# Attention by head pairs, with each pair's rows of the mode weights contracted beside the next pair's attention, and the mix packed by columns

## Chip, cores, metric

The kernel runs on one core of one Trainium2 chip. The metric is device time of one execution in microseconds (us), less is better. "Busy" times and waits come from one profiled execution each. A ratio is the mean time of one kernel's fast runs over the mean of the other's fast runs in the same rounds, so it is not quite the ratio of the medians that are quoted.

The engines are called as the profile calls them: PE (matmul), PEld (its weight load), DVE (vector), ACT (scalar, exponentials), POOL (GpSimd), SP (issues DMAs). "SPq" and "ACTq" are the instruction queues of SP and ACT that issue DMAs. SBUF is the on-chip memory that holds the tiles, PSUM the one that PE writes to here, in banks. The granted clock is the share of PE's full clock that the profile shows as granted in a stretch. The DMA share adds up the time of overlapping packets, so it can pass 1; it came to 1.24 where the weight stream ran steadily.

## The reference, cut to what matters

```python
# attention, 8 batches x 8 heads x 576 positions x 64, feature map of 2 x 128
def phi(x):
    proj = np.einsum('bhsd,df->bhsf', x, w_phi)
    proj = proj - np.max(np.abs(proj), axis=-1, keepdims=True)
    return np.concatenate([np.exp(proj), np.exp(-proj)], axis=-1)
kv  = np.einsum('bhsf,bhsd->bhfd', phi(k), v);  z = phi(k).sum(axis=2)
num = np.einsum('bhsf,bhfd->bhsd', phi(q), kv); den = phi(q) . z
x   = (num / den) as [batch, seq, head*64]          # D = 512

# spectral mix over x: 64 modes, one complex 512 x 512 matrix per mode
X = rfft(x, axis=1)[:, :64]
Y = X . (w_r + i w_i)            # per mode m: [8 batches, 512] x [512, 512]
u = x + irfft(Y);  out = u + relu(u @ w_ch)
```

The mode weights are 2 x 64 x 512 x 512 floats, 134 MB in fp32. Everything else that is read is about 29 MB.

## The kernel before

It has three stages. In the first, 32 units (one batch, two heads) go through attention; after a batch's last unit its Fourier transform is taken. Only when all heads of all batches are done can the mix of a mode start, since each mode needs all 512 rows of the spectrum. The mix loops over the modes, each with two weight transfers of 1 MB (read) and 16 matmuls with 8 stationary columns. The tail inverts the transform and multiplies by `w_ch`.

```python
units = [(b, g) for b in range(B_) for g in range(H_ // 2)]
for (ub, ug) in units:                     # skewed emission: front(n), back1(n-1), back2(n-2)
    f_q.append(frontA(ub, ug))
    if len(f_q) > 1: k_q.append(backA1(f_q.pop(0)))
    if len(k_q) > 1:
        st = k_q.pop(0); backA2(st)
        if st["h1"] == H_ - 1: rfftB1(st["b"])
...
for m in range(NMODES):
    wrr = pw.tile([128, 4, 512], BF16, tag="wrb")    # 6 buffers each
    wir = pw.tile([128, 4, 512], BF16, tag="wib")
    nc.gpsimd.dma_start(wrr, moe_w_r[m].rearrange("(dc p) e -> p dc e", p=128))
    nc.gpsimd.dma_start(wir, moe_w_i[m].rearrange("(dc p) e -> p dc e", p=128))
    ...                                              # 16 matmuls: [128 x 8].T @ [128 x 512]
    nc.scalar.copy(yst[:, 0, :], psYr); nc.vector.tensor_copy(yst[:, 1, :], psYi)
    nc.scalar.dma_start(yall[m:m + 1, :, :], yst[:, 0, :])
    nc.scalar.dma_start(yall[64 + m:65 + m, :, :], yst[:, 1, :])
```

The softmax here doesn't subtract the row's maximum and nothing guards it: scores larger than these inputs give would overflow.

## Time and profile before

Median 776.85 us (3 runs, 776.2 to 777.28).

| stage | us | what fills it |
|---|---|---|
| attention | 0 to about 390 | DVE 81%, ACT 76% busy (100 to 380 us); DMA share 0.33 |
| mix | 390 to 700 | weight stream at 207 GB/s; DVE 14%, ACT 12% |
| last rows of the mix | 700 to 703 | one transfer's landing |
| tail | 703 to 774 | PE 81%, DVE 78% |

The page of the kernel before: busy time of each engine; then the span in 40 slices, where a digit is the busy share in tenths (the rows of DVE and of the DMA), and GB/s moved; then the chain that ended last, by engine and by line.

```profile
PE 535.2 (69%) x3718; PEld 291.4 (38%) x3730; DVE 389.8 (50%) x896; ACT 322.3 (42%) x735; POOL 121.7 (16%) x173
...
DVE  5635889788878878787612111111111111116885
DMA  6899454544443421011089999999999999990445
GB/s 148 147 196 166 113 112 107 113 105 96 111 109 79 99 56 31 17 32 32 1 142 208 207 207 207 207 207 207 208 207 207 207 207 207 207 159 8 163 139 183
...
DMA 43%; issue 21%; PE 11%; DVE 10%; ACT 8%; SPq 5%; POOL 1%; DVEq 0%; POOLq 0%; ACTq 0%
DMA wrr<-in_moe_w_r_dram 36%; PE psf L421 3%; DMA qn<-in_q_dram 3%; DVE vaug L245 2%; DMA vn<-in_v_dram 2%; ACT AkBk L227 1%; ACT XT L322 1%; PE psN L208 1%; DVE ub L397 1%; ACT AkBk L222 1%; SPq L147 1%; DVE mk L214 1%; SPq L148 1%; PE psuT L407 1%; DMA out_dram<-of 1%
```

The two rows DVE and DMA are nearly complements: once DVE is at 7 to 8 tenths the DMA is at 5 tenths at most and falls to 0, and while the DMA is full DVE is at 1 or 2 tenths. The chain says the same: 36% of the span is waiting for weights.

The table of stages of the kernel before (start:end, length, then busy us and instruction count of PE, PEld, DVE, ACT, POOL, then granted PE clock, DMA share, GB/s):

```profile
core 0: us, PE busy (x) PEld busy (x) DVE busy (x) ACT busy (x) POOL busy (x), PEclk, DMA share, GB/s
100.00:380.00 280.00, 192.69 (x1922) 140.34 (x1925) 227.25 (x569) 212.11 (x517) 17.28 (x23) 0.77 0.33 75
400.00:680.00 280.00, 202.48 (x902) 74.10 (x899) 38.70 (x57) 32.55 (x57) 81.47 (x110) 1.00 1.24 207
703.00:774.00 71.00, 57.81 (x354) 29.35 (x360) 55.48 (x96) 13.95 (x24) 0.00 (x0) 0.96 0.38 134
```

In the middle row 280 us of the mix hold 38.7 us of DVE. GB/s counts what is written (bf16); twice that, 414 GB/s, is read.

### The profile page before, as it was taken

The page shows a single profiled execution, that of the slowest core. Times are in us where ns is not written, and L with a number is a line of the kernel's source. Part 1 is how long each engine was busy: PE and PEld are TensorE (multiplying, and loading weights), DVE is VectorE, ACT ScalarE, POOL GpSimd, SP SyncE. Part 2 cuts the span into 40 slices and gives each one's busy share as a digit, 9 for nine tenths or more (in the row PEclk, how much of TensorE's full clock was granted, in tenths as well). Part 3 has the DMA queues.
Part 4 walks back from the last instruction along what each step waited for, and adds up shares of the span by engine and source line. Part 5 has one row for each costly group of instructions (what it writes and reads, how often), then busy time and mean ns, then how long its engine had stood idle before and what let it go on. Part 6 is the DMA issues. An engine that isn't in the chain of part 4 may idle for free.

```text
span 774.3 us, 10671 instructions
## 1 busy us (share of the span) xinstructions
PE 535.2 (69%) x3718; PEld 291.4 (38%) x3730; DVE 389.8 (50%) x896; ACT 322.3 (42%) x735; POOL 121.7 (16%) x173
## 2 busy tenths in 40 slices
PE   1734776667667667776799776676677667667886
PEld 0422554545455444545533222222222222223443
DVE  5635889788878878787612111111111111116885
ACT  2844788877787877865411110110111011012220
POOL 1311010100100000000033323222232322200000
PEclk9855789887967887666599999999999999999999
DMA  6899454544443421011089999999999999990445
GB/s 148 147 196 166 113 112 107 113 105 96 111 109 79 99 56 31 17 32 32 1 142 208 207 207 207 207 207 207 208 207 207 207 207 207 207 159 8 163 139 183
DMA packets 192358, 107.74 MB, mean 139 GB/s; under 512 B 120496, under 2 KB 187184, under 8 KB 192304
## 3 DMA queue, kind: packets, MB, share of 16 engines
q0 software_dynamic: 67584, 67.12, 52.4%
q1 hardware_dynamic: 122672, 38.89, 20.9%
q10 hardware_dynamic: 2048, 1.05, 0.7%
q8 instruction: 29, 0.48, 0.2%
q14 instruction: 25, 0.20, 0.1%
HBM read 163.64 MB, written 9.44 MB: 224 GB/s over the span
## 4 chain that ended last, share of the span: by engine, by line
DMA 43%; issue 21%; PE 11%; DVE 10%; ACT 8%; SPq 5%; POOL 1%; DVEq 0%; POOLq 0%; ACTq 0%
DMA wrr<-in_moe_w_r_dram 36%; PE psf L421 3%; DMA qn<-in_q_dram 3%; DVE vaug L245 2%; DMA vn<-in_v_dram 2%; ACT AkBk L227 1%; ACT XT L322 1%; PE psN L208 1%; DVE ub L397 1%; ACT AkBk L222 1%; SPq L147 1%; DVE mk L214 1%; SPq L148 1%; PE psuT L407 1%; DMA out_dram<-of 1%
## 5 line engine op out<-in xcount | busy, mean ns | idle before, releaser
L384 DVE CAST yst<-psYi 8x512 bf16<-8x512 f32 x64 | 43.5, 679 | 272.7 <-PE psYi L378 272.7
L383 ACT CAST yst<-psYr 8x512 bf16<-8x512 f32 x64 | 36.8, 574 | 275.5 <-PE psYr L368 275.5
L363 PE MATMUL psYr<-wrr,XT 128*8 128x512 bf16 x256 | 66.5, 383 | 82.8 <-DMA wrr<-in_moe_w_r_dram 82.8
L257 PE MATMUL kvzT<-AkBk,vaug 128*65 128x128 bf16 x640 | 63.4, 257 | 22.1 <-DVE vaug L245 20.2
L359 POOL DMA_DIRECT2D wir<-in_moe_w_i_dram x64 | 47.5, 742 | 194.1 <-PE psYi L373 185.8
L368 PE MATMUL psYr<-wir,XT 128*8 128x512 bf16 x256 | 66.6, 383 | 0.0
L363 PEld LDWEIGHTS <-XT 128*8 128x8 bf16 x256 | 17.8, 86 | 129.2 <-DMA wrr<-in_moe_w_r_dram 109.5
L373 PE MATMUL psYi<-wir,XT 128*8 128x512 bf16 x256 | 65.9, 380 | 0.0
L378 PE MATMUL psYi<-wrr,XT 128*8 128x512 bf16 x256 | 65.7, 379 | 0.0
L257 PEld LDWEIGHTS <-vaug 128*65 128x65 bf16 x640 | 53.0, 137 | 29.1 <-DVE vaug L245 24.5
L173 PE MATMUL ptr<-ident_b,tb 128*128 128x128 bf16 x320 | 35.7, 255 | 40.6 <-POOL tb L168 26.1
L358 POOL DMA_DIRECT2D wrr<-in_moe_w_r_dram x64 | 47.6, 744 | 101.6 <-DMA wrr<-in_moe_w_r_dram 86.4
L168 POOL CAST tb<-qn 128x640 bf16<-128x640 f32 x32 | 24.5, 767 | 247.8 <-DMA qn<-in_q_dram 76.6
L214 DVE TENSOR_REDUCE mk<-psN 128x4 f32<-128x512 f32 (+1 forms) x96 | 52.3, 593 | 13.6 <-PE psN L208 13.5
L214 DVE TENSOR_REDUCE mq<-psN 128x4 f32<-128x512 f32 (+1 forms) x96 | 54.2, 581 | 8.3 <-PE psN L208 8.2
L222 ACT ACTIVATE AkBk<-psN 128x512 bf16<-128x512 f32 (+1 forms) x96 | 52.0, 541 | 5.2 <-DVE mk L214 5.2
L227 ACT ACTIVATE AkBk<-psN 128x512 bf16<-128x512 f32 (+1 forms) x96 | 53.0, 552 | 0.0
L173 PEld LDWEIGHTS <-tb 128*128 128x128 bf16 x320 | 27.3, 116 | 51.0 <-POOL tb L168 27.4
L296 DVE TENSOR_TENSOR tB<-psNB,e2mq 128x325 f32<-128x325 f32 x64 | 30.4, 493 | 20.9 <-PE psNB L291 19.6
L245 DVE TENSOR_TENSOR vaug<-vn,emm 128x650 bf16<-128x650 f32 x32 | 26.8, 838 | 24.6 <-ACT emm L239 24.3
L421 PE MATMUL psf<-wchb,uTb 128*128 128x512 bf16 x154 | 35.8, 379 | 0.6 <-DVE of L426 0.3
L368 PEld LDWEIGHTS <-XT 128*8 128x8 bf16 x256 | 22.4, 88 | 33.6 <-issue 1.2
(913 smaller groups left out, 971.7 us busy)
## 6 DMA issues: line engine op xcount, KB each, us to landing
wrr<-in_moe_w_r_dram POOLq DMA_DIRECT2D x64, 512.0 KB, 20.3
wir<-in_moe_w_i_dram POOLq DMA_DIRECT2D x64, 512.0 KB, 20.3
qn<-in_q_dram SPq DMA_DIRECT2D x64, 128.0 KB
kn<-in_k_dram SPq DMA_DIRECT2D x64, 128.0 KB
vn<-in_v_dram SPq DMA_DIRECT2D x64, 128.0 KB
out_dram<-of SPq DMA_DIRECT2D x32, 256.0 KB
yall<-yst ACTq DMA_DIRECT2D x128, 8.0 KB
wchf<-in_moe_w_ch_dram SPq DMA_DIRECT2D x1, 1024.0 KB
```

Of the source, the lines that this page charges most:

```text
L173: nc.tensor.transpose(ptr[:, c * 128:(c + 1) * 128], tb[:, c, :, :].rearrange("p h d -> p (h d)"), ident_b,)
L214: nc.vector.tensor_reduce(out=mm[:, :, 2 * cc:2 * cc + ncc].rearrange("p h c -> p c h"), in_=psN[:, 0:ncc, :].rearrange("p c (h f) -> p c ...
L222: nc.scalar.activation(AkBk[:, 2 * cc:2 * cc + ncc, :, 0, :], psN[:, 0:ncc, :].rearrange("p c (h f) -> p c h f", h=2), ACT.Exp, scale=1.0,)
L227: nc.scalar.activation(AkBk[:, 2 * cc:2 * cc + ncc, :, 1, :], psN[:, 0:ncc, :].rearrange("p c (h f) -> p c h f", h=2), ACT.Exp, scale=-1.0,)
L257: nc.tensor.matmul(kvzT[:, ab * 128:(ab + 1) * 128], lhsT=vaug[:, ab, c, hh, :], rhs=AkBk[:, c, hh, ab, :], start=(c == 0), stop=(c == NCH ...
L358: nc.gpsimd.dma_start(wrr, moe_w_r[m].rearrange("(dc p) e -> p dc e", p=128))
L359: nc.gpsimd.dma_start(wir, moe_w_i[m].rearrange("(dc p) e -> p dc e", p=128))
L363: nc.tensor.matmul(psYr, lhsT=XT[:, dc, 0, m, :], rhs=wrr[:, dc, :], start=(dc == 0), stop=False,)
L368: nc.tensor.matmul(psYr, lhsT=XT[:, dc, 2, m, :], rhs=wir[:, dc, :], start=False, stop=(dc == 3),)
L373: nc.tensor.matmul(psYi, lhsT=XT[:, dc, 0, m, :], rhs=wir[:, dc, :], start=(dc == 0), stop=False,)
L378: nc.tensor.matmul(psYi, lhsT=XT[:, dc, 1, m, :], rhs=wrr[:, dc, :], start=False, stop=(dc == 3),)
L421: nc.tensor.matmul(psf, lhsT=uTb[:, dc, c * 128:(c + 1) * 128], rhs=wchb[:, dc, :], start=(dc == 0), stop=(dc == 3),)
```

## The change

Intent: the contraction over 512 rows is split in four by head pair. Attention now runs pair by pair (for a pair, four units of two batches each, 16 units in all). When a pair is through, its 128 rows of all modes' weights can be contracted, four modes ("a group", 2.1 MB read) at a time, while the next pair's attention runs. Sums over pairs are kept in SBUF (`yacc`). A group's four modes are put in four strips of 32 PE columns. All casts of q and k are done by the DMA. The diff rewrites nearly every line; its core is:

```diff
-    for m in range(NMODES):            # after all attention
-        ... load w_r[m], w_i[m] (512 rows), 16 matmuls of 8 columns
+    def wload(g, mg):                  # a group: 4 modes, 128 rows of pair g; 6 buffers
+        wt = pw.tile([128, 2, MG, DMODEL], BF16, name="wt", tag="wt")
+        for i, w in ((0, moe_w_r), (1, moe_w_i)):
+            nc.gpsimd.dma_start(wt[:, i], w[mg*MG:(mg+1)*MG, g*128:(g+1)*128, :].rearrange("m p e -> p m e"))
+    def mix(g, mg, wt, XT):
+        for i in range(2):
+            for j in range(MG):        # strip j of 32 columns
+                nc.tensor.matmul(py[32*j:32*j+32, :], lhsT=XT[:, t, 4*o+j, 4*i:4*i+4, :]..., rhs=wt[:, i, j, :], ...)
+        if t == 0: return              # two groups share one PSUM bank
+        if g == 0:        nc.scalar.copy(yacc[:, o, :], py)
+        elif g < NG - 1:  nc.vector.tensor_tensor(out=yacc[:, o, :], in0=py, in1=yacc[:, o, :], op=ALU.add)
+        else:
+            nc.vector.tensor_tensor(out=yst, in0=py, in1=yacc[:, o, :], op=ALU.add)
+            for j, t, i ...:           # 16 transfers of 8 rows
+                nc.sync.dma_start(yall[n:n + 1, :, :], yst[r:r + 8, :])
+    units = [(g, bp) for g in range(NG) for bp in range(NP)]
+    for n, u in enumerate(units):
+        front(st[u])                   # transposes, exponentials, maxima
+        st[units[n + 2]] = load(*units[n + 2])
+        next_w(2 if g == 0 else 4)     # request groups of weights
+        back(st.pop(u), XTs[g])        # kv, numerator, division, spectrum
+        for _ in range(4):             # four mixes at the unit's end
+            if mixq: mix(...)
+        if bp == NP - 1: mixq += [(g, mg) for mg in range(NMG)]
+    while mixq: ...                    # the last pair's 16 groups, then the tail
-    psum: 4 buffers of 1 bank, 2 of 1, 1 of 2
+    psum: "one", 4 buffers of 1 bank; "two", 2 buffers of 2 banks
... (tables, layouts of q, k, v, tail: cut)
```

## The prediction

> **What bounds the kernel now.** By the table of stages:
> - Attention, 0 to 390 us. From 100 us DVE is busy 32 to 36 of every 40 us, ACT 30 to 33; DMA share falls from 0.5 to 0. Two e2mq activations lie 10.5 us apart (26 in 105.6 to 367.4 us): a pair of one batch.
> - Mix, 390 to 700 us. Weight DMAs move 207 GB/s of bf16 (414 GB/s read) steadily; DVE and ACT are 11 to 15% busy. The chain of waits gives 36% of the span to "DMA wrr". 134 MB of weights at that rate are an estimated 324 us; 12 of 128 transfers are prefetched.
> - Tail, 703 to 774 us: PE and DVE over 80% busy.
>
> **What the change does.** Weights are loaded by a head pair's rows, in 16 groups (2.1 MB read, about 5.07 us of DMA each) usable while the next pair's attention runs. Only the first pair cannot overlap it (six prefetched groups aside).
>
> DMA after: 64 groups x 5.07 = 324 us. q, k, v add 1.77 MB read per unit (two batches, two heads; 16 units) in descriptors of 1 KB and 256 B: an estimated 5 to 6.5 us. The Trainium skill ("DMA: Bandwidth & Descriptors", "Issuing engines are not separate DMA queues") says that queues share the same 16 engines, so these add. The trace agrees: beside the prefetch attention waits 14.6 us for vn and 12.5 us for qn (chain of waits, 37 to 64 us).
>
> Compute per unit: DVE reductions of 128x512 take 664 ns, so 128x1024 about 1.15 us; with the rest 14 to 15 us. ACT exps start 0.48 us apart at 512 columns, so about 0.9 at 1024: 14 to 16 us. Before, the same work cost 20.9 us for 17 us of DVE. Two double-bank PSUM buffers serve eleven uses per unit, an estimated 17 to 19 us. I expect 20 to 22 us.
>
> The mix's matmuls fall from 1024, 216 ns apart (16 per 3.46 us in the catch-up at 390 us), to 512. The skill ("TensorEngine Tiling (Array Packing)", "Key Properties") says that tiles work independently; no run shows it yet. PE did not bind the mix: little saved. Its evictions fall from 80 us to about 20.
>
> **Sum**
> - start 15, four units of the first pair at 21: 99 us
> - twelve units at the DMA's pace, 4 x 5.07 + 6 = 26.5: 318 us
> - rest of the last pair's weights, 11 x 5.07: 55 us
> - last rows of yall 3, tail 66 (72 before; 36 chunks for 40): 69 us
>
> Total 540 us, range 502 to 590. Faster by over 2%: 0.96; within 2%: 0.02; slower: 0.02.
>
> **What would show it.** DMA near its present rate from 100 to 470 us, weights longest in the chain; a lower DMA share in the first pair; DVE and ACT 55 to 65% busy in the middle; units 26 us apart after the first four; four column-tiled matmuls starting much closer than 216 ns; a tail of 65 to 70 us.
>
> **What would make it wrong.** (1) Coupling: q and k share a FIFO with weights, and weights wait for buffers freed by the mix, so engines may wait in turn: 30 us a unit, 590. (2) Two PSUM double buffers may serialise PE, DVE and ACT: units bound by compute. (3) Small descriptors slower than estimated. (4) Upside: q/k/v at 4 us: 500.

## The result and the profile after

Median 662.58 us (4 runs, 660.45 to 663.73) against 776.53 us, ratio 0.8539 (95% interval 0.8518 to 0.8559). It is clearly faster, and clearly slower than the range of the prediction (502 to 590 us). The same lines of the page of the changed kernel:

```profile
PE 373.7 (56%) x2938; PEld 212.3 (32%) x2957; DVE 281.7 (43%) x452; ACT 252.3 (38%) x432; POOL 209.6 (32%) x288
...
DVE  0644546345344343455545445544440000017755
DMA  6999132331999999999999999996969999100337
GB/s 111 157 189 207 39 49 40 56 36 37 167 181 205 151 210 145 215 141 212 154 186 207 171 216 168 209 183 101 206 104 208 210 210 201 31 10 0 144 144 285
...
PE 36%; ACT 32%; SPq 12%; DVE 10%; POOL 3%; issue 3%; DMA 2%; another core or an unknown queue 0%; DVEq 0%; ACTq 0%; POOLq 0%
SPq L393 12%; ACT AQ L240 9%; PE two L266 6%; PE two L189 6%; PE one L372 6%; ACT AB L214 5%; ACT AB L213 5%; PE one L473 5%; PE one L336 4%; PE two L271 3%; ACT qT L181 3%; DVE ub L456 3%; PE two L287 3%; ACT XT_84 L346 2%; ACT XT_85 L346 2%
```

The weights are gone from the chain. In their place PE and ACT take turns (36% and 32%), and "SPq L393", the issuing of the transfers that write the mix's result, has 12%. DVE, ACT and PE are all around half busy. The table of stages of the changed kernel (units 1 to 3 of pair 0; the twelve units of pairs 1 to 3; the rest of the mix; the wait after it; the tail):

```profile
58.00:139.00 81.00, 49.87 (x394) 34.66 (x396) 39.18 (x60) 42.48 (x73) 20.06 (x28) 0.58 0.36 57
139.00:487.00 348.00, 226.81 (x1928) 133.07 (x1942) 165.41 (x254) 172.65 (x295) 133.08 (x180) 0.63 1.03 167
487.00:567.00 80.00, 20.24 (x160) 4.29 (x152) 6.23 (x9) 2.47 (x4) 20.76 (x28) 0.54 1.15 193
567.00:592.00 25.00, 0.83 (x5) 0.19 (x5) 0.69 (x1) 0.00 (x0) 0.00 (x0) 0.50 0.05 12
592.00:662.00 70.00, 56.95 (x324) 27.08 (x326) 46.71 (x72) 18.26 (x36) 0.00 (x0) 0.96 0.35 136
```

In the first row three units take 81 us, 27.0 us each, for 39.18 us of DVE, 42.48 of ACT and 49.87 of PE: 13.1, 14.2 and 16.6 us per unit. No engine is near its limit and the DMA is at 57 GB/s. The work of DVE and ACT was estimated about rightly (14 to 15 us of DVE, 14 to 16 of ACT), that of PE was not estimated at all; that it would pack into 20 to 22 us was wrong. One unit of the changed kernel in order of time (start, us, engine, line, operation, output<-inputs, shapes, and in brackets the idle time before and what ended it; equal rows are merged):

```profile
111.07 1.18 ACT L181 COPY kT<-one 128x640 bf16<-128x640 bf16 x2 [5.45 <-PE one L180]
111.82 1.89 PE L189 MATMUL two<-w2blk,kT 128*128 128x256 bf16 x8 [0.20 <-ACT kT L181]
112.89 2.36 DVE L193 TENSOR_REDUCE mk<-two 128x8 f32<-128x1024 f32 x2 [1.15 <-PE two L189]
114.81 2.44 ACT L346 CAST XT_84<-one 128x128 bf16<-128x128 f32 x4 [2.56 <-PE one L340]
116.75 1.35 ACT L213 ACTIVATE AB<-two 128x1024 bf16<-128x1024 f32 x1
...
121.52 2.65 DVE L221 TENSOR_TENSOR va<-vn,ee 128x1152 bf16<-128x1152 f32 x2 [5.94 <-ACT ee L216]
122.22 0.58 PE L233 MATMUL two<-qT,w2blk 128*128 128x512 bf16 x1 [6.42 <-ACT qT L181]
123.27 3.77 ACT L240 ACTIVATE AQ<-two 128x1024 bf16<-128x1024 f32 x4 [0.61 <-remote]
...
132.02 0.59 ACT L275 CAST kvz<-two 128x520 bf16<-128x520 f32 x1 [2.41 <-PE two L271]
```

The unit is a relay. ACT copies kT, PE computes the k products, DVE reduces them, ACT takes exponentials (116.75 to 121.2 us), DVE waits 5.94 us for `ee` and multiplies `va`, PE waits 6.42 us for `qT`, ACT takes the q exponentials (3.77 us), PE forms kv, ACT copies it, PE forms the numerators. Only the first steps of the next unit run earlier, beside the end of this one: the row at 114.81 us is ACT copying the spectrum of the unit before, which ends at 117.2 us, 6 us after this unit's kT copy began.

The drain of the changed kernel, from the last unit to the tail (the row 502.35 is a merged row: 128 issues on SP's queue in 87.94 us):

```profile
502.35 87.94 SPq L393 DMA_DIRECT2D yall<-yst  x128
...
539.56 0.69 DVE L387 TENSOR_TENSOR yst<-one,yacc 128x512 bf16<-128x512 f32 x1 [10.30 <-DMA yall<-yst]
...
566.95 0.62 PE L372 MATMUL one<-wt,XT_85 128*32 128x512 bf16 x4 [2.09 <-DMA wt<-in_moe_w_i_dram]
569.54 0.69 DVE L387 TENSOR_TENSOR yst<-one,yacc 128x512 bf16<-128x512 f32 x1 [7.49 <-DMA yall<-yst]
591.74 3.90 PE L447 MATMUL one<-yall,CI 128*128 128x512 bf16 x8 [24.17 <-DMA yall<-yst]
```

The weights end at 567 us, but DVE (its copies out of PSUM are called evictions) sits idle 7.5 to 14.6 us before six of its eight evictions, for buffers that the transfers hold (63.0 us in all), SP issues for 88 us with hardly a pause (81.5 us busy), and PE waits 24.17 us more. The 88 us also start late. The first eviction ends at 492.9 us, the first issue comes at 502.35: `yall` is allocated in one of the six weight buffers (`tag="wt"`), and the first issue waits for the matmuls that end at 502.3 us. What these 9.5 us cost is seen in the last run below.

### The profile page after: what moved, and what is told of

The parts are those of the page before. It is cut to its first block, busy times and chain, and to the rows that moved or that the text cites. A ratio compares the mean times of both kernels' runs of the same rounds, so it can differ in the third digit from the quotient of the medians.

```text
span 661.9 us, 7649 instructions
## 1 busy us (share of the span) xinstructions
PE 373.7 (56%) x2938; PEld 212.3 (32%) x2957; DVE 281.7 (43%) x452; ACT 252.3 (38%) x432; POOL 209.6 (32%) x288
## 4 chain that ended last, share of the span: by engine, by line
PE 36%; ACT 32%; SPq 12%; DVE 10%; POOL 3%; issue 3%; DMA 2%; another core or an unknown queue 0%; DVEq 0%; ACTq 0%; POOLq 0%
SPq L393 12%; ACT AQ L240 9%; PE two L266 6%; PE two L189 6%; PE one L372 6%; ACT AB L214 5%; ACT AB L213 5%; PE one L473 5%; PE one L336 4%; PE two L271 3%; ACT qT L181 3%; DVE ub L456 3%; PE two L287 3%; ACT XT_84 L346 2%; ACT XT_85 L346 2%
## 5 line engine op out<-in xcount | busy, mean ns | idle before, releaser
L356 POOL DMA_DIRECT2D wt<-in_moe_w_r_dram x64 | 49.3, 770 | 91.7 <-PE one L372 71.7
L221 DVE TENSOR_TENSOR va<-vn,ee 128x1152 bf16<-128x1152 f32 x32 | 42.3, 1365 | 68.0 <-ACT ee L216 68.0
L372 PE MATMUL one<-wt,XT_85 128*32 128x512 bf16 x256 | 33.6, 561 | 59.8 <-DMA wt<-in_moe_w_i_dram 30.7
L240 ACT ACTIVATE AQ<-two 128x1024 bf16<-128x1024 f32 x64 | 61.3, 1090 | 2.4 <-remote 2.4
L193 DVE TENSOR_REDUCE mk<-two 128x8 f32<-128x1024 f32 x32 | 37.7, 1220 | 54.1 <-PE two L189 54.1
L356 POOL DMA_DIRECT2D wt<-in_moe_w_i_dram x64 | 49.5, 774 | 17.5 <-DMA wt<-in_moe_w_i_dram 16.7
L266 PE MATMUL two<-va,AB 128*128 128x65 bf16 x512 | 51.9, 244 | 0.0
L193 DVE TENSOR_REDUCE mq<-two 128x8 f32<-128x1024 f32 x32 | 39.2, 1225 | 21.2 <-PE two L189 21.2
L287 PE MATMUL two<-kvz,AQ 128*128 128x65 bf16 x512 | 35.8, 241 | 22.0 <-ACT kvz L275 10.9
L189 PE MATMUL two<-w2blk,kT 128*128 128x256 bf16 x128 | 24.1, 352 | 23.9 <-ACT kT L181 23.8
L346 ACT CAST XT_84<-one 128x128 bf16<-128x128 f32 x32 | 19.6, 991 | 46.8 <-PE one L340 46.8
L163 POOL DMA_DIRECT2D qb<-in_q_dram x32 | 23.6, 738 | 40.8 <-DMA wt<-in_moe_w_r_dram 30.6
L346 ACT CAST XT_85<-one 128x128 bf16<-128x128 f32 x32 | 19.6, 993 | 40.3 <-PE one L340 40.3
```

Source lines behind the costliest of these rows:

```text
L163: eng.dma_start(t[:, 8 * i:8 * i + 8, :].rearrange("p (h c) d -> p h (c d)", h=2), hs[:, 0:512, :].rearrange("h (p c) d -> p h (c d)", c=4),)
L189: nc.tensor.matmul(ps[:, 2 * j:2 * j + 2, :].rearrange("p c f -> p (c f)"), lhsT=tT[:, 4 * i + j, :], rhs=w2blk, start=True, stop=True,)
L193: nc.vector.tensor_reduce(out=m[:, 8 * i:8 * i + 8], in_=ps, axis=AX.X, op=ALU.max, apply_absolute_value=True,)
L221: nc.vector.tensor_tensor(out=va[:, ab, :, 0:64], in0=st["vn"], in1=ee[:, ab, :].unsqueeze(2).to_broadcast([128, 18, 64]), op=ALU.mult,)
L240: nc.scalar.activation(AQ[:, ab, i], ps, ACT.Exp, scale=1.0 - 2.0 * ab)
L266: nc.tensor.matmul(o, lhsT=AB[:, ab, n, :], rhs=va[:, ab, n, :], start=(c == 0), stop=False,)
```

## The experiments

The theory after the traces: (A) a unit is bound by its own serial chain, not by the DMA; (C) the drain is bound by issuing 128 small transfers on one queue; (D) the start is late because POOL's queue is serial. Together these are the missing 120 us. Rivals: (B) units are paced by weights, or by q and k behind them in one FIFO; (A2) two double-bank PSUM buffers serialise front and back whatever the order.

### No weight stream (one run, result wrong)

```diff
-                wts[key] = wload(*key)
+                if len(kept) < 5: kept.append(wload(*key))   # five groups, loaded once
+                wts[key] = kept[...]                           # used for all 64 mixes
```

> Five groups of weights are loaded once and used for all 64 mixes (wrong result on purpose), so the weight stream is gone and all compute stays. Theory A (a unit is bound by its own serial chain of PE, ACT and DVE, with the mix in it): units of head pairs 1 to 3 keep their spacing, 27 to 30 us. Rival B (units are paced by the weight stream, or by q and k queued behind it): units of pairs 1 to 3 fall to 24 us or less, at most the 27 us of pair 0. The rest after the last unit shrinks under both, as no weights are awaited.

655.99 us, one run, state unknown; all eight runs of the kernel before on this chip were 774 to 778 us and fast. The copy of kv (once per unit) in the changed kernel, then in this one (count, min/median/max ns, first and last start):

```profile
L275 ACT CAST kvz<-two x16: 592/592/592, 51.0 to 479.9; 128x520 bf16<-128x520 f32 x16
```

```profile
L275 ACT CAST kvz<-two x16: 592/593/593, 51.1 to 480.2; 128x520 bf16<-128x520 f32 x16
```

And the stage table's row of the twelve units in the run without weights:

```profile
139.00:487.00 348.00, 226.84 (x1924) 133.49 (x1938) 165.43 (x254) 172.70 (x295) 69.36 (x92) 0.63 0.23 35
```

Taking 59 of 64 groups away moved the last unit by 0.3 us. Rival B falls: with the DMA at 35 GB/s the twelve units take about the same 348 us, and DVE and ACT work is equal to 0.1 us. The whole run is only about 7 us shorter, since the drain without any weight to wait for is still held by the issuing, which only begins 8 us earlier (494.2 against 502.35 us); its evictions waited as long as before (waits of this run):

```profile
DVE yst L388 <- DMA yall<-yst: 62.9, 6, 11.6
```

So in the drain two limits lay side by side, 76 us of weights and 88 us of issuing (in the changed kernel begun 9.5 us late), and the longer one ended it.

The same row sizes the loads of q, k and v, the only ones left: 0.23 of 348 us is 80 us for ten units, an estimated 6.5 us per unit of a stream at share 1.24. The prediction's 5 to 6.5 us, which it gives without a source, holds at its upper end; its warning (3), slower small descriptors, is not the cause.

### The next unit's front ahead of this unit's back

```diff
-        front(st[u])
+        front(st[units[n + 1]])        # front of unit 0 ahead of the loop
         next_w(2 if g == 0 else 4)
         back(st.pop(u), XTs[g])
```

> The front part of the next unit is emitted ahead of the back part of this one. Theory A1 (order of emission makes the chain serial): pair-0 units fall from 27 to about 21 us, and the total by 20 to 50 us. Rival A2 (the two double-bank PSUM buffers serialise front and back whatever the order): less than 1 us per unit, total within 2%.

667.7 us, ratio to before 0.8584 (0.857 to 0.8598): 0.5% above the changed kernel's 0.8539, so the same by the 2% rule. Units of pair 0 kept 26.9 us. So shifting a whole front past a whole back is not enough. The text on record would have given this result to the PSUM buffers; the next two runs show that it is not theirs alone.

### Three double-bank PSUM buffers

```diff
-    ps1 = tile_pool("ps1", bufs=4);  ps2 = tile_pool("ps2", bufs=2)
+    ps1 = tile_pool("ps1", bufs=2);  ps2 = tile_pool("ps2", bufs=3)
```

> Three double-bank and two single-bank PSUM buffers in place of two and four; the order of emission is untouched. Rival A2 (PSUM buffers): pair-0 units fall from 27 to 23 us or less, total faster by 20 us or more. Theory A1 (order of emission): less than 1.5 us per unit; fewer single banks may cost a little.

684.39 us, ratio 0.8797 (0.8776 to 0.8818), slower. Pair 0's units did fall, from 27.0 us to between 23.3 and 23.8 us, so the buffers are part of the chain. But units that hold a mix settled at 30.6 us, with the single banks halved; over the run they cancel out: the first and last copy of kv lie 431.3 us apart, 428.9 in the changed kernel. Most of the 22 us that the run lost lie elsewhere, in the tail, which uses single banks alone: 87 us in place of 70, at a granted clock of 0.76 in place of 0.96 (compare the last row of the changed kernel's table):

```profile
596.00:683.00 87.00, 72.69 (x324) 32.25 (x328) 48.31 (x72) 20.37 (x36) 0.00 (x0) 0.76 0.28 109
```

So the total is no fair test of rival A2; the unit time of pair 0 is, and it speaks for A2 and against the pure form of A1. Both order and buffers make the relay.

### Front and back in alternation

Front and back are cut in four (kT copy | k exponentials and `va` | q exponentials | q maxima, and kv | numerators of batch 0 | of batch 1 | rest and spectrum) and emitted in turn, front of the next unit first. PSUM is as in the changed kernel.

```diff
+        f = front(st[units[n + 1]]); b = back(st.pop(u), XTs[g])   # generators
+        next(f); next(b); next(f); next(b); next(f); next(b); next(f)
         ... loads, next_w ...
+        next(b)
```

> Front of the next unit and back of this one are cut in four and emitted in alternation, PSUM buffers as in the changed kernel. Theory A1: pair-0 units of 18 to 21 us, units of pairs 1 to 3 then at the pace of the DMA, about 26 us; total faster by 40 to 60 us. Rival A2 (PSUM buffers): pair-0 units stay above 25 us, total within 2%.

612.56 us, ratio 0.7878 (0.7866 to 0.789), 50 us faster than the changed kernel. The copy of kv, then the chain of this run:

```profile
L278 ACT CAST kvz<-two x16: 592/592/594, 50.3 to 418.6; 128x520 bf16<-128x520 f32 x16
```

```profile
DMA 22%; PE 22%; ACT 20%; SPq 13%; DVE 10%; POOL 6%; issue 3%; another core or an unknown queue 2%; ACTq 0%; DVEq 0%; POOLq 0%
DMA wt<-in_moe_w_i_dram 22%; SPq L398 13%; PE one L489 5%; ACT AB L214 4%; ACT AB L215 4%; ACT XT L351 4%; PE one L377 3%; PE two L269 3%; DVE va L222 3%; POOL wt L361 3%; ACT AQ L242 2%; DVE ub L472 2%; PE two L274 2%; ACT uT L481 2%
```

The last unit comes 61 us earlier. Pair 0's units take 22.1 us and the rest 22 to 29 us, 25.4 on average. Weights are back at the head of the chain (22%; "another core or an unknown queue" and "remote" are releases that the profile could not place, there is one core): now the DMA is near its pace in the middle (198 GB/s from 160 to 430 us, against 207 in the old mix), as the prediction had it for the changed kernel. That it sets the pace is read from the trace; no run took the weights out of this kernel. Like the run with the whole front ahead of the back, this one also loads q, k and v one unit earlier, which gained nothing there. It also shows that 22.1 us per unit is possible with two double-bank buffers.

### Half the small transfers on ACT's queue

```diff
-    nc.sync.dma_start(yall[n:n + 1, :, :], yst[r:r + 8, :])
+    (nc.sync if i == 0 else nc.scalar).dma_start(yall[n:n + 1, :, :], yst[r:r + 8, :])
```

> Only change: of the 128 transfers that write the mix's result into its rows, half are issued from ACT's queue in place of SP's. Theory C (the drain is bound by issuing: 128 x 0.69 us = 88 us on one queue): the gap between the last matmul of the mix and the first of the tail falls from 24 us to 6 us or less, and the total by 18 to 24 us; the drain then takes the 75 us of the weights. Rival (each transfer's landing, or the two buffers in front of it, is the limit whatever the queue): less than 5 us.

649.49 us, ratio 0.8355 (0.8329 to 0.8382): 13 us faster, where 18 to 24 were expected. The transfers by queue (each issue still 627 to 634 ns) and the first matmul of the tail:

```profile
L393 SPq DMA_DIRECT2D yall<-yst x64: 634/634/800, 502.5 to 574.4; - x64
L393 ACTq DMA_DIRECT2D yall<-yst x64: 627/627/1224, 502.5 to 574.1; - x64
L448 PE MATMUL one<-yall,CI x32: 376/376/631, 576.8 to 609.5; 128*128 128x512 bf16 x32
```

The last matmul of the mix begins at 568.0 us (567.0 before), so the drain now ends with the weights, and the gap to the tail is 8.2 us in place of 24.2. Of these 8.2 us, eight issues on each queue are 5.0 us and the last eviction 0.7; the rest I take for landing. The size was over-estimated (the gap is 8.2 us and not 6, the weights end 1 us later, and the tail is 1 us longer); the theory stands, the rival's "less than 5 us" does not. The Trainium skill ("Perfetto Trace Analysis", "What 'DMA-bound' means") lists as one kind of DMA-bound the issuing engine's track being solid DMA slices. The trace agrees: in the changed kernel 128 slices, 81.5 us in all, lie in 87.94 us of SPq. The same page ("DMA Optimizations") advises to balance such issues over the engines that can make them, and this run agrees, with 13 us.

### An earlier start

```diff
+    iotas; st = {units[0]: load(*units[0])}
     for x in XTb: nc.gpsimd.memset(x, 0.0)       # was ahead of all loads
-    st = {both first units}; wchb load; tables()
+    st[units[1]] = load(*units[1]); wchb load
     ... front(unit 0)
+    tables()                                     # emitted behind the first front
```

> Only change: at the start, GpSimd's small index patterns and the first unit's q and k come ahead of the two 3.5 us memsets and of the second unit's loads, and the sine tables are emitted behind the first unit's front. Theory D (the late start of PE, 29 us, is serial work on GpSimd's queue): PE starts at 12 to 17 us, all units shift by as much, total faster by 10 to 16 us. Rival (the drain or the DMA takes the gain back): units start earlier but the total moves by less than 5 us.

646.15 us, ratio 0.8321 (0.8286 to 0.8355), 16 us faster. The first PE work in the changed kernel, then here:

```profile
29.38 1.09 PE L134 MATMUL one<-ident_f,yacc 128*128 128x128 f32 x4 [29.38 <-ACT yacc L118]
```

```profile
8.88 0.61 PE L171 MATMUL one<-ident_b,kb 128*128 128x128 bf16 x4 [8.88 <-DMA kb<-in_k_dram]
```

PE starts at 8.9 us, earlier than expected, and the first kv copy moves from 51.0 to 34.8 us. In the changed kernel PE's queue began with transposes of tables that waited for index patterns, which sat on POOL's queue behind two memsets of 3.5 us and 16 loads of q and k; attention queued behind them. The run moved loads, memsets and tables at once, so their shares are not told apart.

### The mix not packed (one run, result wrong)

```diff
-    py[32*j:32*j+32, :]
+    py[32*j:32*j+32, :] if t == 0 and i == 0 else py[0:32, :]   # 12 of 16 matmuls in strip 0
```

> Three of every four rounds of the mix's matmuls write to the same 32 columns in place of four strips (wrong result on purpose), so they cannot run side by side; all else stays. If the mix sits in the units' serial chain (theory A): units of pairs 1 to 3 grow by 5 to 9 us each, 24 serial matmuls at 0.22 to 0.43 us less what they took packed, total slower by 50 to 100 us. Rival (PE has room, as the prediction held: packing saves little): less than 2 us per unit.

682.83 us, one run, state unknown, 20 us slower. (The comparison with the reference passed all the same: the spectral part is small beside the attention output, so it isn't a sharp test of the mix.) One unit's mixes in the changed kernel, then here:

```profile
427.85 1.03 PE L372 MATMUL one<-wt,XT_84 128*32 128x512 bf16 x5
429.14 2.32 PE L372 MATMUL one<-wt,XT_84 128*32 128x512 bf16 x20
432.57 0.78 PE L372 MATMUL one<-wt,XT_84 128*32 128x512 bf16 x7
```

```profile
440.34 1.04 PE L372 MATMUL one<-wt,XT 128*32 128x512 bf16 x5
441.64 2.43 PE L372 MATMUL one<-wt,XT 128*32 128x512 bf16 x6
444.65 4.06 PE L372 MATMUL one<-wt,XT 128*32 128x512 bf16 x21
```

These 32 matmuls, with the spectrum's matmuls that lie between them, take 5.5 us packed and 8.4 us unpacked (over the units 4.2 to 5.5 us, and 8.4 to 8.8), and the units of pairs 1 to 3 settle at 30.7 us in place of 28 to 31. The truth lies between: packing is on the chain, which the prediction denied, but worth 20 us, not 50 to 100. That strips run side by side is plain in the drain, where the granted clock is 0.50 in both runs: packed, the four matmuls of 512 columns of a transfer start within 0.01 us and end within 0.62 us of the first's start; in one strip they start 0.38 to 0.43 us apart (581.17, 581.55, 581.98, 582.40 us in this run) and take 1.86 us. This agrees with the Trainium skill ("TensorEngine Tiling (Array Packing)", "Key Properties"), by which tiles execute independently.

### All three together, then with the mixes spread

```diff
# e7: alternation + early start + two queues.  e10, on top:
-        for _ in range(4): one mix              # at the unit's end
+        one mix after each of the unit's four steps
```

> The alternating emission, the early start and the two queues together. Alone, alternation gave 50 us. Theory: the unit's chain, the start and the issue-bound drain were the three losses, and they add: about 612 less 13 less 24, so 570 to 580 us, with units of pairs 1 to 3 at the pace of the weights and the drain ending with the weights. If the gains overlap: 590 to 600 us.

> On top of e7: one mix after each of a unit's four steps in place of four at its end, the first at the head of the pair's next unit. In e7 the six weight buffers are full from about 85 to 135 us and the DMA moves 50 GB/s, since the first mix comes at the end of the fifth unit. Theory E (the stream restarts a unit late; the DMA is the limit from then on): the stream restarts 15 to 20 us earlier, the weights end as much earlier, total 560 to 568 us against 581. Rival (the units' chain takes it back: mixes wait for weights inside a unit and hold up its attention): 575 us or more.

e7: 581.14 us, ratio 0.7497 (0.7461 to 0.7533). The three gains of 50, 16 and 13 us add (79 us; measured 81). The total lies just above the 570 to 580 us expected, which counted 24 us for the two queues. Its table of stages, for the end of pair 0 and the middle:

```profile
85.00:135.00 50.00, 26.67 (x278) 18.83 (x276) 30.53 (x45) 29.72 (x52) 14.88 (x20) 0.74 0.37 54
140.00:400.00 260.00, 163.05 (x1686) 98.58 (x1677) 145.88 (x220) 145.65 (x248) 111.84 (x159) 0.78 1.22 198
```

For 50 us the DMA moves 54 GB/s: six buffers are full and the first mix, which frees them, comes at the end of the fifth unit. From 140 to 400 us the stream runs at nearly its rate. e10: 571.93 us, ratio 0.7362 (0.7327 to 0.7397). The first matmul of the mix moved from 137.0 to 127.0 us and the total by 9 us: the direction of theory E, half of its size. Some units now last 28 to 33 us, but the weights end 11.6 us earlier (487.3 against 498.9 us for the last matmul).

### Two rows per transfer

```diff
-    16 transfers: yall[n:n + 1, :, :] <- yst[r:r + 8, :]
+     8 transfers: yall[n:n + 65:64, :, :] <- yst[r:r + 16, :]    # SP for even groups (t == 0), ACT for odd
```

> On top of e10: each transfer into the mix's rows writes two rows, so 64 in place of 128, over the two queues. If issuing still costs at the end, the gap between the last matmul of the mix and the first of the tail falls from 8 us to about 5, total 2 to 4 us faster than e10; if what is left is landing, no change. It may also turn out that one transfer can't write two rows this way, and the result is wrong.

586.47 us, ratio 0.7531 (0.7511 to 0.7552), correct, but 15 us slower than e10. The gap before the tail did fall, from 8.2 to 5.9 us, but the last mix came at 508 us in place of 487, with single waits for weights of 4 to 5 us between the batches of these transfers. A possible reason is that such a transfer uses fewer of the 16 engines: the Trainium skill ("DMA: Bandwidth & Descriptors", "Why a DMA increments its semaphore by 16 and not by 1") says that the number of engines must divide the size of the slowest dimension that is not 1, here 2 in place of 8. The trace agrees as far as it goes. From 487 to 508 us, with the last weights issued by 482 us, the mix still waits for weights while the DMA does little:

```profile
487.00:508.00 21.00, 3.09 (x20) 0.57 (x20) 0.69 (x1) 0.00 (x0) 0.00 (x0) 0.50 0.15 31
```

The share of 0.15 is about an eighth of the 1.24 of a full stream, as if two of 16 engines still had work. No row names an engine, so the cause is likely and not shown.

### The change without its overlap (one run, result wrong)

```diff
-        for _ in range(4): if mixq: mix(...)     # all 64 mixes behind the last unit
-        next_w(2 if g == 0 else 4)
+        next_w(2 if n < 3 else 0)                # six groups prefetched
```

> The changed kernel with the overlap alone taken out: all 64 mixes come behind the last unit, six groups of weights are prefetched as before (the spectra of pairs 0 and 1 are overwritten by then, so the result is wrong on purpose). If the change's new attention is no faster than the old one and all its gain is overlap, the total is slower than the kernel before: last unit at about 465 us (16 units of 27 us behind a start of 29), 58 groups of 5.07 us to about 760, the write of the last rows and the tail to 840 to 860 us. If the new attention or the packed mix carries part of the gain: below 776 us.

852.08 us, within the 840 to 860 us expected; one run, state unknown (the kernel before in the same job: 776.64). Its attention and mix stages:

```profile
0.00:460.00 460.00, 263.90 (x2114) 182.36 (x2133) 219.39 (x356) 227.94 (x384) 125.21 (x173) 0.61 0.37 57
470.00:750.00 280.00, 66.89 (x436) 12.47 (x436) 15.22 (x22) 2.92 (x5) 78.49 (x106) 0.50 1.24 207
```

The new attention ends at about 460 us, 70 us later than the old one; the mix then runs at the old pace of 207 GB/s. So the overlap is worth 852 - 663 = 189 us, and all of the gain: what else the change did costs 75 us against the kernel before. Where those 75 us sit follows from the traces. The first matmul of the mix comes 72.5 us later than in the old kernel (457.8 against 385.3 us): the first product with `w_phi` starts at 32.7 us in place of 22.0, and the units take 26 to 27 us where the old kernel spent 20.9 for the same work in its middle. The mix itself is 8 us shorter (306.6 against 314.5 us), and the gap before the tail is 10 us longer (13.8 against 3.6 us).

This run also tells what `yall` in a weight buffer costs in the changed kernel. Here the first issue follows the first eviction at once, and the rest of the drain is alike (76.4 us from the first eviction to the last matmul, 75.4 there):

```profile
L393 SPq DMA_DIRECT2D yall<-yst x128: 634/635/802, 688.8 to 776.1; - x128
```

The gap before the tail is 13.8 us in place of 24.2, so by this run about 10 of the 24 us come from the late start of the issuing and 14 from the issuing itself and the last landing.

### All runs

| kernel | us | ratio to before |
|---|---|---|
| before | 776.5 | 1 |
| the change | 662.6 | 0.854 |
| e1 coarse shift of emission | 667.7 | 0.858 |
| e2 three double-bank buffers | 684.4 | 0.880 |
| e3 early start | 646.2 | 0.832 |
| e4 two queues | 649.5 | 0.836 |
| e5 no weight stream (wrong) | 656.0 | one run |
| e6 alternation | 612.6 | 0.788 |
| e7 = e3 + e4 + e6 | 581.1 | 0.750 |
| e9 mix not packed (wrong) | 682.8 | one run |
| e10 = e7 + mixes spread | 571.9 | 0.736 |
| e11 = e10 + two rows per transfer | 586.5 | 0.753 |
| e12 no overlap (wrong) | 852.1 | one run |

e10 beats both kernels.

## Why the prediction was wrong

The direction and the reason for the gain were right: the overlap of attention and weights is what pays (e12). The size was wrong by 122 us. Its sum, term by term, measured in the trace of the changed kernel (a unit ends with its last copy of the spectrum: 63.3 us for unit 0, 144.2 for unit 3, 491.5 for unit 15):

| term of the sum | predicted | measured | tested by |
|---|---|---|---|
| start and first unit (15 + 21) | 36 | 63.3 | e3: 16 us of it is the order on POOL's and PE's queues |
| three more units of pair 0 | 63 | 81.0 | e6: 22.1 us per unit |
| twelve units "at the DMA's pace" | 318 | 347.2 | e5: same without weights |
| rest of the last pair's weights | 55 | 76.1 | e7, e10: the stream restarts late |
| last rows of yall | 3 | 24.2 | e4: 8.2 with two queues; e12: 13.8 with issuing begun in time |
| tail | 66 | 70.2 | e2: 87.1 with two single banks |
| sum | 541 | 662 | |

Point by point:

- **"I expect 20 to 22 us [per unit]" failed; this is the step that broke the sum.** The work of DVE and ACT was sized about rightly (13.1 us of DVE, 14.2 of ACT; PE, with 16.6 us the busiest, was not sized) but turned into time as the old kernel did it, which has its front and back skewed over three units. The new emission has one unit's front and back one after the other, and the trace shows a relay of 27.0 us. With alternation the figure is 22.1 us (e6). The signs that the prediction had named fail with it: the DMA moved 167 GB/s from 139 to 487 us, not 207, the weights left the chain, and DVE and ACT were 48% and 50% busy there, not 55 to 65%.
- **"Twelve units at the DMA's pace" failed for that reason.** Units of 28 to 31 us are slower than the stream's pace, so the stream waits for the units. e5 settles it: without the stream the units keep their times. Once the units are quick (e6) the predicted pace does appear: 25.4 us on average against 26.5.
- **Warning (1), coupling of q, k and weights in one FIFO, with its "30 us a unit", named the right size for a wrong cause.** e5 rules it out. Warning (2), the PSUM buffers, was the nearer one: with three buffers pair 0 fell to about 23.5 us (e2), but order alone does as much (e6).
- **"Rest of the last pair's weights, 11 groups" was mis-sized.** It measured 76.1 us, which at 5.07 us is 15 groups (120 of the mix's 512 matmuls, 15 groups' worth, start in it). The sum let the stream run at full pace from the end of pair 0; the buffers are in fact freed one unit later, at the end of the fifth unit (e7: 50 us at 54 GB/s). Spreading the mixes won back 9 us.
- **"Last rows of yall 3" failed.** The kernel before issued the same 128 transfers at 627 ns each, but over 310 us. Here they come in the last 76 us, 88 us of issuing on one queue, and `yall` in a weight buffer lets them start 9.5 us late (14 and 10 us of the gap by e12). The count and the buffer were in the diff and the 627 ns in the trace; the prediction did not multiply them.
- **"Start 15" failed**, by the order on POOL's and PE's queues (e3).
- **"PE did not bind the mix: little saved" was partly wrong.** It held for the old mix. In the new kernel the mix sits inside a serial chain, so its PE time counts: unpacked costs 20 us (e9).
- **The tail (65 to 70 us, measured 70.2) and a lower DMA share in pair 0 were about right**, and so was the claim about strips.

What stays open: how much of a unit's 27 us comes from the granted PE clock, which was 0.58 in pair 0 against 0.77 in the old attention (0.74 to 0.78 with alternation). A lower clock lengthens PE's part of the chain (one 512-column matmul starts 0.43 us after another at 0.50 in e9's drain, 0.216 us at 1.00 in the old mix), and no run separated clock from order. PE's busy share does not explain the clock by itself: 62% busy in pair 0 at 0.58, 53% at 0.74 in e7 (85 to 135 us), 72% at 1.00 in the old mix. The reason for e11's loss is likely but not shown. Why e2's tail took 17 us more, the banks or the lower clock, is open too.

## What to carry to other kernels

Here the overlap of two stages moved the limit to the slower stage's dependency chain, not to its busiest engine. When no engine and no queue is near full, sum the chain and look at the order of emission before counting work. After such a change, look at what used to be spread over the hidden stage (here 128 small transfers at 0.63 us) and now comes in one burst, and at what shares a buffer with the stream (here `yall`). To learn whether a stream is on the critical path, take it away: if nothing moves, it was not.

## What the Trainium skill lacked or had wrong

- "DMA: Bandwidth & Descriptors", "Issuing engines are not separate DMA queues": it says that issuing from several engines only saves the sequencer's time, "which is usually small relative to the DMA itself". For transfers of 8 KB it was the limit of the drain here: 634 ns per issue, 128 in 87.94 us on one queue, and two queues saved 13 us of 663. "Perfetto Trace Analysis", "DMA Optimizations", has it right: it advises balancing over the issuing engines where the track of one is full of issues.
- "DMA: Bandwidth & Descriptors" has a latency to the first byte, but no time for how long one issue holds the queue of SP or ACT (a table in its part on trn3 has a count of cycles for "previous generations", without their clock); the runs show 627 to 635 ns for 8 KB transfers, in the kernel before and after.
- "TensorEngine Tiling (Array Packing)": the section "PSUM Bottleneck" and the theoretical speedup don't tell what packing is worth inside a serial chain; here 12 of every 16 matmuls unpacked cost 20 us of 663 (one run).
- No page has a figure for what the order of emission is worth: the same work with the same buffers took 27.0 us per unit emitted part by part, and 22.1 us emitted in alternation.
